# A fused attention and gated-FFN kernel on one core: where the closing waits stand, and when one add of the last block is planned

## The chip, the cores and the metric

The kernel runs on one core of a Trainium2 chip. A core has a matmul engine (PE; its weight loads are listed as PEld), a vector engine (DVE), an activation engine (ACT), GpSimd (POOL), and a sync engine (SP) that here issues every transfer between device memory (HBM) and the on-chip buffer (SBUF). Engines run their own instruction streams and meet at semaphores. The metric is the device time of one execution in microseconds (us), as the median of several runs.

## The reference

All tensors are bf16. `x` has 2048 rows of 576.

```python
x = A_x
xn = _layernorm(x, axis=-1)
s = _A_ref(xn, A_wqkv, A_wo)          # 32 heads of 18, causal, window of 256, softmax, then @ wo
g = _silu(_B_ref(xn, B_w_gate, B_w_up, B_w_down))
return x + s * g

def _B_ref(x, w_gate, w_up, w_down):
    g = jnp.einsum("bsd,df->bsf", x, w_gate)      # 576 -> 4608
    u = jnp.einsum("bsd,df->bsf", x, w_up)
    h = _sigmoid(g) * u
    return jnp.einsum("bsf,fd->bsd", h, w_down)   # 4608 -> 576
```

## The kernel before, in words

The 2048 rows go through in four chunks of 512 rows, each of four blocks of 128. For each chunk the program does: the layer norm on DVE; transposition, so that features lie on partitions (`xn`); the projection to q, k and v on PE (L460); attention in units of heads and keys (scores L589, exponential on ACT L607, masks on DVE L625, values L658); the output projection (L734), whose result ACT copies as a quarter of itself to `sat`; the FFN's two first matrices in 36 slices of 128 columns (L777), each followed by a tanh on ACT (L763) and a multiply on DVE (L767) into `hT`; and the FFN's second matrix, block by block (L851), accumulated over all 36 slices in PSUM.

A block ends in `final_cols` (from L904). Sigmoid and silu are made of tanh, and the factors of two are folded into scales. Four operations follow each other on a block's PSUM result y: ACT's tanh(y/4) into `thf` (L912, named fth), DVE's (t + 1) y (L914, fq1), DVE's product with `sat` (L916, fq2), and DVE's add of x in the tile `xf` (L918, fq3). Then SP stores `xf` to the output. The rows of x for `xf` are loaded anew by `load_xf`.

The last block of the last chunk has its own builder, `build_last` (L870). It makes the block in two column pieces, 0 to 448 (the large piece) and 448 to 576 (the small one): all 36 matmuls of the large piece, then all 36 of the small one (L881), each followed by its own `final_cols`, so its own four operations and its own store. Both pieces share one load of `xf`.

The order of the instructions on each engine is not written by hand. The builder makes a list of operations, each with an engine, an assumed duration, a priority and what it depends on. `schedule` (L924) is a planner: it repeatedly places, of the operations whose predecessors are placed, the one that can start first on its engine by the assumed times, with priorities as small penalties. The order of placing on an engine is the order of the program there. For a transfer the planner assumes an end by a bandwidth, and its `slack` is a further time that it adds before the operations that need the data count as ready. The slack is in no instruction; it moves only the plan. For the loads of `xf` it is LATE_SLACK, 5000 ns; the usual value for a transfer is DMA_SLACK_NS, 600 ns. SP's queue is planned in the same way.

`emit` (L1047) writes the program. Every transfer belongs to a lane, which is a semaphore of its own that rises by 16 per transfer; there are 84 lanes, one per ring buffer and kind of transfer. In front of each operation `run_engine` writes a wait for every semaphore that the operation needs and that the engine does not yet know to be high enough (`known`, kept per engine). The two stores of the last block are the last two transfers on SP; the large one goes through a lane that blocks before it used too, the small one through a lane of its own. At the end of SP's stream all 84 lanes are waited for, in a loop without regard to `known`:

```python
            if e == "SP":
                for ln, v in enumerate(lane_cnt):
                    if v > 0:
                        eng.wait_ge(lanes[ln], v)
                eng.nop()
```

In the built program these waits are mostly put two to an instruction: 41 wait instructions listed under L1095, one under L1096, and a single wait on the branch behind them (L1098). Then come a drain of each engine and a barrier of all of them.

Of the kernel before, what the change touches and what calls it, by code (L numbers as in the profile page):

```python
# [19 lines left out]
NFT = F // P  # L20
# [35 lines left out]
FB_CUTS = (0,3,6)  # L56
LAST = 448
W_GATE = 2
F2B = ((0, 1), (2, 3), (6, 7), (4, 5))
PVB = ((0,), (1,), (2,), (3,))  # L60

# [2 lines left out]
DMA_SLACK_NS = 600.0  # L64
# [8 lines left out]
LATE_SLACK = 5000.0  # L73
# [18 lines left out]
def mm_ns(n):  # L92
    return max(28.0, n / 2.4 + 2.5)
# [76 lines left out]
class Builder:  # L170
# [583 lines left out]
    def build_ffn(self, c):  # L754
# [82 lines left out]
        for blocks in (((0, 1), (2,), (3,)) if c == 0 else ((0,), (1,), (2,), (3,))):  # L837
            cands = F2B if blocks[-1] == QPC - 1 else ((6, 7), (4, 5), (0, 1), (2, 3))
            banks = {i: Psum(*cands) for i in blocks}
# [3 lines left out]
            for q in range(NWD):  # L843
                for i in blocks:
# [17 lines left out]
                    f2_ops[(i, q)] = o  # L862
                    if i == W_GATE and q == 0:
                        w_gate = o
# [5 lines left out]
    def build_last(self, c, prev):  # L870
        i = QPC - 1
        sb = c * QPC + i
        sth, dth = self.r_th.take()
        sx, o_x = self.load_xf(sb)
        for n, (c0, c1) in enumerate(((0, LAST), (LAST, D))):
            ps = Psum((6,), (7,), (4,), (5,), (0,), (1,), (2,), (3,))
            for q in range(NWD):
                def f_f2(e, q=q, ps=ps, c0=c0, c1=c1):
                    for fl in range(WDG):
                        ft = q * WDG + fl  # L880
                        r = e.matmul(self.bank(ps, c1 - c0), self.hT[:, ft, i * P:(i + 1) * P],  # L881
                                     self.wd_sb[:, q, fl, c0:c1], start=(ft == 0), stop=(ft == NFT - 1))
                    return r
                deps = [self.op_hT[ft] for ft in range(q * WDG, (q + 1) * WDG)] + [self.op_wd[q]]
                o = self.op("PE", WDG * mm_ns(c1 - c0), f_f2, f"f2:{sb}:{q}:{n}", deps, 3, alloc=[ps] if q == 0 else [],
                            mode="full", odeps=prev + ([self.op_wop[i - RTH]] if q == 0 else []))
                ps.users.append(o)
                prev = [o]
            ss, o_s = self.op_s[i]
            self.final_cols(sb, ps, o, sth, dth, ss, o_s, sx, o_x, c0, c1)  # L890

    def load_xf(self, sb):
        sx, dx = self.r_xf.take()
        return sx, self.dma(self.xf[:, sx, :], self.x[sb * P:(sb + 1) * P, :], P * D * 2, f"xf{sb}", ("xf", sx),
                            deps=dx + [self.op_hT[NFT - 6]], prio=3, slack=LATE_SLACK)

    def build_final(self, sb, ps, o_f2, sth, dth, ss, o_s):
        sx, o_x = self.load_xf(sb)
# [148 lines left out]
    def emit(self):  # L1047
        nc = self.nc
        ENGS = ("PE", "ACT", "DVE", "POOL", "SP")
        for o in self.ops:  # L1050
            if o.lane is not None:
                o.needs_tok = True
            for d in o.deps:
                d.needs_tok = True
        lanes = [nc.alloc_semaphore(f"lane{i}") for i in range(len(self.lane_ids))]
        lane_cnt = [0] * len(lanes)
        cnt = {e: 0 for e in ENGS}
        for e in ENGS:
            for o in self.prog[e]:
                if not o.needs_tok:  # L1060
                    continue
                if o.lane is not None:
                    ln = self.lane_ids[o.lane]
                    lane_cnt[ln] += 16
                    o.tok = (("L", ln), lane_cnt[ln])
                else:
                    cnt[e] += 1
                    o.tok = (("E", e), cnt[e])

        def semof(key):  # L1070
            return lanes[key[1]] if key[0] == "L" else self.sem[key[1]]

        def run_engine(e, eng):
            known = {}
            for o in self.prog[e]:
                waits = {}
                for d in o.deps:
                    k, v = d.tok
                    if e == "PE" and d.eng == "PE" and d is not o.fence:
                        continue  # L1080
                    if waits.get(k, -1) < v:
                        waits[k] = v
                for k, v in waits.items():
                    if known.get(k, -1) >= v:
                        continue
                    known[k] = v
                    eng.wait_ge(semof(k), v)
                ins = o.fn(eng)
                if o.needs_tok:
                    k, v = o.tok  # L1090
                    ins.then_inc(semof(k), 16 if o.lane is not None else 1)
            if e == "SP":
                for ln, v in enumerate(lane_cnt):
                    if v > 0:
                        eng.wait_ge(lanes[ln], v)  # L1095
                eng.nop()  # L1096

        with nc.Block() as block:  # L1098
            @block.tensor
            def _(eng):  # L1100
                run_engine("PE", eng)

            @block.scalar
            def _(eng):
                run_engine("ACT", eng)

            @block.vector
            def _(eng):
                run_engine("DVE", eng)

            @block.gpsimd
            def _(eng):
                run_engine("POOL", eng)

            @block.sync
            def _(eng):
                run_engine("SP", eng)
# [42 lines left out]
```

## Time and profile before

| what | value |
|---|---|
| time, median of 3 runs | 570.92 us (570.83 to 571.53) |
| the profiled execution, its own time | 571.24 us |
| its span, first to last instruction | 569.0 us |
| PE busy in the span | 560.6 us (99%) |
| DVE, ACT, POOL busy | 304.8, 274.7, 28.2 us |
| granted PE clock | 1.00 |
| DMA traffic | 73.03 MB, mean 128 GB/s |

Times in the profile are counted from the start of the span. A page cuts the span in 40 slices and gives each engine's busy share per slice in tenths. A timeline line has the start, the duration, the engine, the source line, the operation with what it writes and reads, and in brackets how long the engine was idle before it and who released it. "SPq" and the like mark an engine's sequencer: instructions that issue transfers, wait or branch, which do not count as busy time. "DMA to landing" is the time from the start of the issuing instruction to the last increment of its semaphore.

### The profile page before, as it was taken

How to read it: one execution, taken by the hardware profiler on the slowest of the kernel's cores; microseconds unless marked ns; L12 is line 12 of the kernel's file. 1: busy time of each engine (PE TensorE's matmuls, PEld its weight loads, DVE VectorE, ACT ScalarE, POOL GpSimd, SP SyncE). 2: the span in 40 equal slices, each digit the busy share in tenths (PEclk: the TensorE clock that was granted, in tenths of full speed). 3: DMA queues.
4: the chain of work that ended last, by engine and by line, in shares of the span. 5: the costliest groups of instructions: out<-in, count | busy, mean ns of one | idle time of the engine just before them, and what ended most of it. 6: DMA issues, size and time to landing. Idle time of an engine off the chain costs nothing.

```text
span 569.0 us, 17867 instructions
## 1 busy us (share of the span) xinstructions
PE 560.6 (99%) x7854; PEld 284.3 (50%) x7854; DVE 304.8 (54%) x664; ACT 274.7 (48%) x372; POOL 28.2 (5%) x55
## 2 busy tenths in 40 slices
PE   8999999999999999999999999999999999999996
PEld 5634444457544444456654444545754444444543
DVE  6137888732137896661205788765121586675312
ACT  7456666314055856721307576580321856856011
POOL 3000100010000100010000010001000000000100
PEclk9999999999999999999999999999999999999999
DMA  8999998528946765234694665604479455640001
GB/s 198 204 204 250 240 219 204 124 61 117 203 91 145 160 142 136 64 57 92 101 223 95 147 149 125 150 25 73 87 147 176 104 129 122 154 106 23 20 22 43
DMA packets 124874, 73.03 MB, mean 128 GB/s; under 512 B 53630, under 2 KB 124286, under 8 KB 124798
## 3 DMA queue, kind: packets, MB, share of 16 engines
q1 hardware_dynamic: 124798, 71.90, 59.5%
q8 instruction: 62, 1.02, 0.8%
q14 instruction: 14, 0.11, 0.1%
HBM read 55.22 MB, written 2.36 MB: 101 GB/s over the span
## 4 chain that ended last, share of the span: by engine, by line
PE 94%; SPq 2%; DMA 2%; issue 0%; ACT 0%; DVE 0%; DVEq 0%
PE ps L777 50%; PE ps L851 23%; PE ps L460 8%; PE ps L589 5%; PE ps L658 3%; PE ps L734 3%; SPq L210 2%; PE ps L881 2%; DMA wqkv_sb<-in_A_wqkv_dram 1%; DMA wgs<-in_B_w_up_dram 1%; ACT expr L509 0%; DVE xf L918 0%; DVE thf L914 0%; ACT thf L912 0%; DVE thf L916 0%
## 5 line engine op out<-in xcount | busy, mean ns | idle before, releaser
L777 PE MATMUL ps<-xn,wgs 64*128 64x512 bf16 x2592 | 298.8, 377 | 1.2 <-DMA wgs<-in_B_w_up_dram 1.1
L777 PEld LDWEIGHTS ps<-xn,wgs 64*128 64x128 bf16 x2592 | 120.8, 94 | 146.1 <-issue 9.8
L607 ACT ACTIVATE expr<-ps 128x1024 bf16<-128x1024 f32 x152 | 147.2, 1022 | 28.2 <-PE ps L589 28.2
L851 PE MATMUL ps<-wd_sb,hT 128*128 128x512 bf16 (+1 forms) x1080 | 134.4, 286 | 0.0
L763 ACT ACTIVATE tring<-ps 128x512 bf16<-128x512 f32 x144 | 86.3, 599 | 78.6 <-PE ps L777 63.6
L767 DVE SCALAR_TENSOR_TENSOR hT<-tring,ps 128x512 bf16<-128x512 bf16 x144 | 97.5, 677 | 28.5 <-PE ps L777 27.4
L851 PEld LDWEIGHTS ps<-wd_sb,hT 128*128 128x128 bf16 x1080 | 68.0, 98 | 65.7 <-DVE expr L625 1.7
L625 DVE TENSOR_TENSOR expr<-expr,m 128x512 bf16<-128x512 bf16 (+2 forms) x152 | 58.3, 412 | 61.8 <-ACT expr L607 61.0
L912 ACT ACTIVATE thf<-ps 128x576 bf16<-128x576 f32 (+2 forms) x17 | 10.6, 623 | 139.4 <-PE ps L851 132.2
L914 DVE SCALAR_TENSOR_TENSOR thf<-thf,ps 128x576 bf16<-128x576 bf16 (+2 forms) x17 | 12.2, 718 | 104.9 <-ACT thf L912 104.9
L460 PE MATMUL ps<-wqkv_sb,xn 64*128 64x288 bf16 x864 | 54.7, 283 | 0.6 <-DMA wqkv_sb<-in_A_wqkv_dram 0.6
L460 PEld LDWEIGHTS ps<-wqkv_sb,xn 64*128 64x128 bf16 x864 | 42.9, 94 | 11.3 <-issue 1.9
L589 PE MATMUL ps<-qkp 18*64 18x320 bf16 (+4 forms) x1472 | 32.4, 259 | 0.0
L589 PEld LDWEIGHTS ps<-qkp 18*64 18x64 bf16 x1472 | 16.1, 103 | 32.5 <-issue 15.7
L508 DVE CAST pk<-ps 128x576 bf16<-128x576 f32 x15 | 11.3, 755 | 23.0 <-PE ps L460 22.9
L698 DVE STREAM_TRANSPOSE op__63<-pk 128x512 bf16<-128x512 bf16 x32 | 22.3, 696 | 0.3
L636 POOL COPY qkp<-qkp 128x256 bf16<-128x256 bf16 x24 | 9.6, 398 | 248.6 <-PE ps L589 248.6
L676 DVE STREAM_TRANSPOSE pk<-ps 128x512 f32<-128x512 f32 x32 | 21.6, 675 | 0.0
L658 PEld LDWEIGHTS ps<-expr,vau 64*32 64x32 bf16 x1440 | 17.9, 92 | 6.4 <-issue 5.6
L658 PE MATMUL ps<-expr,vau 64*32 64x320 bf16 (+5 forms) x1440 | 20.7, 253 | 0.0
L674 DVE STREAM_TRANSPOSE tf<-ps 128x512 f32<-128x512 f32 x16 | 11.4, 713 | 15.4 <-PE ps L658 15.1
L734 PE MATMUL ps<-wo_sb,oT 64*128 64x512 bf16 (+1 forms) x288 | 18.7, 283 | 0.1
(52 smaller groups left out, 189.1 us busy)
## 6 DMA issues: line engine op xcount, KB each, us to landing
wgs<-in_B_w_gate_dram SPq DMA_DIRECT2D x48, 240.0 KB, 3.9
wgs<-in_B_w_up_dram SPq DMA_DIRECT2D x48, 240.0 KB, 4.7
wgs<-in_B_w_up_dram SPq DMA_DIRECT2D x48, 192.0 KB, 4.1
wgs<-in_B_w_gate_dram SPq DMA_DIRECT2D x48, 192.0 KB, 4.3
wd_sb<-in_B_w_down_dram SPq DMA_DIRECT2D x9, 576.0 KB, 6.3
xf<-in_A_x_dram SPq DMA_DIRECT2D x18, 144.0 KB, 2.2
out_dram<-xf SPq DMA_DIRECT2D x15, 144.0 KB, 1.9
xr<-in_A_x_dram SPq DMA_DIRECT2D x14, 144.0 KB, 4.2
```

The source lines that it names most:

```text
L460: r = e.matmul(self.bank(ps, HV, hf), self.xn[r0:r0 + 64, k, i * P:(i + 1) * P], self.wqkv_sb[r0:r0 + 64, j, k, :], start=(k == 0), stop=( ...
L589: r = e.matmul(self.ps[64 * half:64 * half + 64, b:b + n * 64], self.qkp[r0:r0 + DH, hg, k0:k0 + 64], self.qkp[r0:r0 + DH, hg, q0 * 64:(q0 ...
L607: return e.activation(self.expr[:, es, 2 * pr:2 * pr + 2, :], src, ACTF.Exp, scale=SM_SCALE)
L625: return e.tensor_tensor(ap, ap, m, ALU.mult)
L658: r = e.matmul(self.ps[32 * j:32 * j + 32, b + q0 * 64:b + (q0 + n) * 64], vf[:, v0:v0 + 32], self.expr[p0:p0 + 64, es, j, pos * 64:(pos + ...
L676: t3 = self.rd("DVE", dve_ns(CH), lambda e, tg=tg, hg=hg: e.transpose(tg, self.bank(ps2[hg][1])), f"t3:{c}:{hg}", deps=[o, self.last_mul] ...
L698: t2 = self.op("DVE", dve_ns(CH), lambda e, on=on: e.transpose(self.op_[:, hg % NOT, :], on.rearrange("p g d -> p (g d)")), f"t2:{c}:{hg}" ...
L734: r = e.matmul(self.bank(ps2[w], n1 - n0, n), self.oT[r0:r0 + 64, kt, qi * P:(qi + 1) * P], self.wo_sb[r0:r0 + 64, kt, n0:n1], start=(swap ...
L763: return e.activation(self.tring[:, st_, :], self.bank(ps), ACTF.Tanh, scale=0.5)
L767: return e.scalar_tensor_tensor(self.hT[:, ft, :], self.tring[:, st_, :], 1.0, self.bank(ps), ALU.add, ALU.mult)
L777: return e.matmul(self.bank((pg, pu)[gu][ft]), self.wgs[r0:r0 + 64, slots[ft // FG], i, fl * P:(fl + 1) * P], self.xn[r0:r0 + 64, i, :], s ...
L851: r = e.matmul(self.ps[:, b + n0:b + n1], lhsT, self.wd_sb[:, q, fl, n0:n1], start=(ft == 0), stop=(ft == NFT - 1))
```

## The change

It has two parts. First, on SP, the waits for all lanes but those of the last two stores (LAST_OUTS = 2) are written in front of the first of these stores, and noted in `known`. The loop at the end waits only for lanes that are not yet noted. Second, in `build_last` the load of `xf` has the slack DMA_SLACK_NS in place of LATE_SLACK, so that the planner takes its data to be ready 4400 ns earlier. In the built program this changes one place: on DVE the add of the large piece (L918) stands ahead of the small piece's L914 and L916, where before it stood behind them.

```diff
 LAST = 448
 W_GATE = 2
+LAST_OUTS = 2
@@ build_last
         sth, dth = self.r_th.take()
-        sx, o_x = self.load_xf(sb)
+        sx, o_x = self.load_xf(sb, DMA_SLACK_NS)
@@
-    def load_xf(self, sb):
+    def load_xf(self, sb, slack=LATE_SLACK):
         sx, dx = self.r_xf.take()
         return sx, self.dma(self.xf[:, sx, :], self.x[sb * P:(sb + 1) * P, :], P * D * 2, f"xf{sb}", ("xf", sx),
-                            deps=dx + [self.op_hT[NFT - 6]], prio=3, slack=LATE_SLACK)
+                            deps=dx + [self.op_hT[NFT - 6]], prio=3, slack=slack)
@@ emit
         def run_engine(e, eng):
             known = {}
+            end = [o for o in self.prog[e] if o.lane is not None][-LAST_OUTS:]
             for o in self.prog[e]:
+                if e == "SP" and o is end[0]:
+                    for ln, v in enumerate(lane_cnt):
+                        if v > 0 and not any(self.lane_ids[d.lane] == ln for d in end):
+                            eng.wait_ge(lanes[ln], v)
+                            known[("L", ln)] = v
                 waits = {}
@@
             if e == "SP":
                 for ln, v in enumerate(lane_cnt):
-                    if v > 0:
+                    if v > 0 and known.get(("L", ln), -1) < v:
                         eng.wait_ge(lanes[ln], v)
                 eng.nop()
```

## The prediction

> **What bounds the kernel now.** I read the engines and the 40 slices first: the matmul engine is busy for 560.6 of 569.0 us, at full clock, so the body belongs to it and neither edit touches an instruction of it. Only the last slice falls off. That slice is where the change acts, so I went on to the end of the span.
>
> ```profile
> span 569.0 us, 17867 instructions
> ...
> PE 560.6 (99%) x7854; PEld 284.3 (50%) x7854; DVE 304.8 (54%) x664; ACT 274.7 (48%) x372; POOL 28.2 (5%) x55
> ...
> PE   8999999999999999999999999999999999999996
> ...
> out_dram<-xf SPq DMA_DIRECT2D x1, 112.0 KB, 1.7
> ...
> out_dram<-xf SPq DMA_DIRECT2D x1, 32.0 KB, 1.6
> ```
>
> The timeline of the end comes next (columns: start, duration, engine, line, operation). PE ends at 563.96. Behind it run ACT, DVE and two stores, and the last one here is issued by 565.99. The span, however, ends at 569.0.
>
> ```profile
> 562.56 0.62 DVE L914 SCALAR_TENSOR_TENSOR thf<-thf,ps 128x448 bf16<-128x448 bf16 x1 [5.54 <-ACT thf L912]
> 562.79 1.17 PE L881 MATMUL ps<-wd_sb,hT 128*128 128x128 bf16 x18
> ...
> 563.22 0.39 DVE L916 TENSOR_TENSOR thf<-thf,sat 128x448 bf16<-128x448 bf16 x1
> 563.99 0.28 ACT L912 ACTIVATE thf<-ps 128x128 bf16<-128x128 f32 x1 [1.47 <-PE ps L881]
> 564.30 0.29 DVE L914 SCALAR_TENSOR_TENSOR thf<-thf,ps 128x128 bf16<-128x128 bf16 x1 [0.69 <-ACT thf L912]
> 564.62 0.22 DVE L916 TENSOR_TENSOR thf<-thf,sat 128x128 bf16<-128x128 bf16 x1
> 564.77 0.52 DVE L918 TENSOR_TENSOR xf<-xf,thf 128x448 bf16<-128x448 bf16 x2
> 565.18 0.81 SPq L210 DMA_DIRECT2D out_dram<-xf  x2
> ```
>
> The chain of waits says nothing of the 3 us behind that, since semaphore instructions do not count as busy. The view by source line shows them: first the closing waits (L1095, L1096), then the end of the program (L1098), with durations in ns and start times.
>
> ```profile
> L1095 SPq EVENT_SEMAPHORE  x41: 17/28/28, 566.0 to 568.5; - x41
> ...
> L1096 SPq EVENT_SEMAPHORE  x1: 28/28/28, 568.5 to 568.5; - x1
> ...
> L1098 SPq COMPARE_BRANCH  x1: 46/46/46, 568.6 to 568.6; - x1
> L1098 SPq DRAIN  x1: 13/13/13, 568.8 to 568.8; - x1
> ```
>
> The reader is to see a queue: 42 wait instructions on SP from 566.04 to 568.57, so 2.53/42 = 0.060 us from one to the next (28 ns is only their recorded part). The last store (issued 565.55) landed 1.57 us later, at 567.12. From then to 568.57, 1.45 us, SP only works off waits that have long been met. From the last of them to the end of the span (branch, drain, barrier of all engines) it is 569.01 - 568.57 = 0.44 us.
>
> The profiled execution took 571.24 us: its span of 569.01 and 2.23 around it. It stands 0.32 above the median of the runs, 570.92. I make the sum against the span and take the difference to the median.
>
> **Part 1, the add of the large piece.** In the built program the only instructions that change place are on DVE: the 448-column add (L918) now stands before the small piece's two operations. PE, ACT and POOL keep their order and their waits.
> - Its cost: the multiply before it ends at 563.22 + 0.39 = 563.61; 0.03 us is the gap between such neighbours (563.18 to 563.22 above); it takes 0.38 (0.52 for both adds, overlapped). So it runs from 563.64 to 564.03, in DVE time that is idle now (563.61 to 564.30; 0.69 in the row). The small piece's first DVE operation waits for ACT until 564.27 and keeps its 564.30, with 0.24 us of cover. Without that cover the small chain would move by what is missing, at most 0.38.
> - The add gets a second wait (the load of xf and the multiply; before, the token of the later multiply covered it). The extra instruction is one semaphore wait for the load, which stands ahead of the wait for the multiply and is met at 561.1; cost 0, or 0.06 if it is not decoded early.
> - What the last store gains: its add no longer stands behind the large one. It starts at 564.85 + 0.03 = 564.88 instead of 565.07, ends at 565.10 (0.22), and its store is issued 0.03 later, as the large one is now (565.15 to 565.18): at 565.13. Today it starts at 565.55, because SP is still at the large store (565.18 to 565.51). That is 0.43 earlier. The large store is now issued at 564.11 to 564.44, clear of it.
> - Landing: as the second of two stores back to back it takes 1.57. The pair of the block before shows what being second costs: 1.76 for the first, 1.88 for the second, and 0.34 against 0.43 for the issue. So alone I take 1.57 - 0.12 = 1.45 us; bounds are 1.45 and 2.16, the latter from the load of xf at 558.96, the slowest transfer of this stretch. I keep near the store rows, since they have the same direction and a like shape. Landing: 566.58.
>
> **Part 2, the waits ahead of the large store.** What moves is 82 of the 84 lanes' waits, two to an instruction, with the store's own wait for DVE in the last instruction: 41 of them stand between the load of xf (issued 558.96, SP free at 559.30) and the large store. Queued behind them on SP are only the two stores; no other engine waits for SP there, and no transfer is issued between.
> - The 22nd waits for that load's lane and is met when it lands, 558.96 + 2.16 = 561.12. By pace it would be reached at 559.3 + 21 x 0.06 = 560.6, so SP stands 0.5 us there. 19 more at 0.06 follow: done at 562.3. The add that the large store needs ends at 564.03. So the cover is 1.7 us, and before the last store is touched another 565.13 - 564.44 = 0.69 us. I cost the moved waits at nothing; if every one of the 19 cost 0.06 us more, still nothing, with 0.15 each the cover is just used up.
> - What is left at the end: one wait instruction for the small store's lane, and the other lane's wait on the branch, whose store lands near 564.11 + 1.7 = 565.8. SP goes on about 0.02 us after a landing (the load of xf was issued at 558.96, the landing that it waited for was at 558.94), 0.03 for the wait, then the 0.44 of before: 566.58 + 0.05 + 0.44 = 567.07.
>
> **The sum.** 569.01 - 567.07 = 1.94 us off the span. Apart: the add alone would let the queue of waits begin at 565.13 + 0.33 = 565.46 instead of 565.99, 0.53 off; the waits alone would give 567.12 + 0.05 + 0.44 = 567.61, 1.40 off. 570.92 - 1.94 = 568.98, said as 569.0, 0.34% faster.
>
> A rule of the Trainium skill speaks against so quick a landing: "DMA: Bandwidth & Descriptors", section "Anatomy of one DMA", gives about 2.0 us of fixed cost for a transfer, most of it the receipt of the write, though measured on the other way of issuing (by GpSimd). By that figure, as an estimate, the small store would land at 565.13 + 2.08 = 567.21 and the gain would be 1.31 us (569.61). The trace of before has 1.57 for this very store, so I go by the trace.
>
> **The rivals.**
> 1. *The store's landing takes the place of the waits.* If the lone small store takes the 2.16 us of the load, the end is 565.13 + 2.16 + 0.05 + 0.44 = 567.78, 1.23 off: 569.7. For it: once the waits are gone, the landing ends last with no cover at all. Against it: every store of the last 25 us landed in 1.6 to 1.9, and DMA is nearly idle (0.17 of the 16 engines at the end).
> 2. *The add does not help, the waits do.* If the small chain is held up by the large add (its cover is 0.24 us) or the stores meet anyway, only the 1.40 is left: 569.5. Against it: 0.38 of work goes into a hole of 0.69.
> 3. *Slower: the moved waits hold up the large store.* Its place is SP between 561.12 and 564.03. Behind it the last store follows at 0.43 us, then landing (1.57) and closing (0.49). To end 1.14 us after 569.01 the large store would have to start at 570.15 - 0.49 - 1.57 - 0.43 = 567.66: the 19 waits would cost (567.66 - 561.12)/19 = 0.34 us each. Then 572.1. Against it stand 42 such waits in a row at 0.060.
> 4. *The body drifts.* Another program on other addresses; the three runs of before lie 0.7 us apart. If that eats half the gain, the time is 570.0, nearer to no change than to a measurable one.
>
> **How the numbers follow.** This kernel's measurement tells about 0.2%, 1.14 us, from no change. My forecast (both parts work; 568.4 to 569.4) 0.60, rival 2 0.14, rival 1 0.10, rival 4 0.12, rival 3 0.04. Faster by over 0.2% (below 569.78): forecast, rival 2, and nearly all of rival 1, which lies at the bound with its 569.7 (0.08 of 0.10): 0.82. Same: rival 4 and the rest of rival 1: 0.14. Slower: 0.04. The range reaches down to 568.3 (the forecast with the runs' spread of 0.7 below the middle) and up to 569.9, which takes in rivals 1 and 2 and leaves out most of 4 and all of 3, near 0.17 with the lower tail.
>
> **What would show it.** Right: the semaphore instructions of the closing waits stand between 559 and 562.5 us, one is left behind the last store; the 448-column add starts near 563.6, right after its multiply; the large store's issue is near 564.1, the small one's near 565.1 with 0.33 us of its own; the span is near 567.1 and ends 0.5 us after the last landing. Wrong: a gap of SP between the last moved wait and a DVE add already done (rival 3); the small piece's first DVE operation more than 0.05 after its activation (rival 2); a landing near 2.1 us (rival 1); PE's end away from 563.96 by more than 0.3 us (rival 4), which would make the prediction wrong without touching its steps.

## The result, and the profile after

The changed kernel takes 569.5 us (median of 22 runs, 568.31 to 572.41) against 570.95 us (22 runs of before, 570.31 to 572.1). The ratio is 0.9975 with a 95% interval of 0.9966 to 0.9985, so 0.25% or 1.4 us faster. The profiled execution took 569.1 us with a span of 566.9.

The timeline of its end, from the large piece's activation on (columns as before):

```profile
561.82 0.54 ACT L913 ACTIVATE thf<-ps 128x448 bf16<-128x448 f32 x1 [5.72 <-PE ps L882]
...
563.05 0.39 DVE L917 TENSOR_TENSOR thf<-thf,sat 128x448 bf16<-128x448 bf16 x1
563.47 0.39 DVE L919 TENSOR_TENSOR xf<-xf,thf 128x448 bf16<-128x448 bf16 x1
563.83 0.28 ACT L913 ACTIVATE thf<-ps 128x128 bf16<-128x128 f32 x1 [1.47 <-PE ps L882]
563.96 1.34 SPq L211 DMA_DIRECT2D out_dram<-xf  x2
564.14 0.29 DVE L915 SCALAR_TENSOR_TENSOR thf<-thf,ps 128x128 bf16<-128x128 bf16 x1 [0.27 <-ACT thf L913]
564.46 0.23 DVE L917 TENSOR_TENSOR thf<-thf,sat 128x128 bf16<-128x128 bf16 x1
564.72 0.23 DVE L919 TENSOR_TENSOR xf<-xf,thf 128x128 bf16<-128x128 bf16 x1
```

The 448-column add now follows its multiply at once and ends 0.27 us before the small piece needs DVE. The two stores, which stood back to back within 0.81 us, now spread over 1.34.

The view by source line of the same kernel (moved waits L1081, one more together with the store's own wait for DVE L1094, the wait left at the end L1103, the end of the program L1105):

```profile
L1081 SPq EVENT_SEMAPHORE  x40: 27/28/28, 559.2 to 562.1; - x40
...
L1094 SPq EVENT_SEMAPHORE  x1: 27/27/27, 563.9 to 563.9; - x1
...
L1103 SPq EVENT_SEMAPHORE  x1: 17/17/17, 566.4 to 566.4; - x1
...
L1105 SPq COMPARE_BRANCH  x1: 46/46/46, 566.5 to 566.5; - x1
L1105 SPq DRAIN  x1: 12/12/12, 566.7 to 566.7; - x1
```

and of the small store alone (L211):

```profile
L211 SPq DMA_DIRECT2D out_dram<-xf x1: 332/332/332, 565.0 to 565.0; - x1
...
DMA to landing us min/median/max: 1.5/1.5/1.5
```

Forty wait instructions have gone into the time in which SP only stood by, and the one left at the end follows the small store's landing (issued 564.97, landed 566.43 by the trace's landing times, 1.46 us) within 0.02 us.

To compare runs I take the *tail*: from the start of the small piece's activation, the last one on ACT, to the end of the span. It leaves out all that happens ahead of it. It was 569.01 - 563.99 = 5.02 us and is 566.91 - 563.83 = 3.08 us. That is 1.94 less, the size that was forecast. The medians, however, lie only 1.45 apart. So there were two questions: do the two parts give what the sum said, and does the body ahead of the tail take 0.5 us back?

| kernel | small piece's activation starts | tail | ratio to before, 95% interval |
|---|---|---|---|
| before | 563.99 | 5.02 | |
| before, again | 563.76 | 5.02 | 0.9996 (0.9983 to 1.0008) |
| changed | 563.83 | 3.08 | 0.9975 (0.9966 to 0.9985) |
| changed, again | 563.68 | 3.07 | 0.9967 (0.9953 to 0.9980) |
| changed, a third time | 563.84 | 3.08 | 0.9965 (0.9952 to 0.9977) |
| waits only | 563.13 | 3.67 | 0.9969 (0.9955 to 0.9983) |
| add only | 564.38 | 4.50 | 0.9992 (0.9980 to 1.0003) |
| waits ahead of the last store alone | 563.90 | 4.90 | 1.0002 (0.9984 to 1.0021) |
| half of the waits moved | 564.14 | 3.20 | 0.9969 (0.9957 to 0.9980) |

Each ratio is against runs of before that were taken alongside.

### The profile page after: what moved, and what is told of

The parts are those of the page before. It is cut to its first block, busy times and chain, and to the rows that moved or that the text cites. A ratio compares the mean times of both kernels' runs of the same rounds, so it can differ in the third digit from the quotient of the medians.

```text
span 566.9 us, 17841 instructions
## 1 busy us (share of the span) xinstructions
PE 557.1 (98%) x7827; PEld 283.8 (50%) x7854; DVE 305.4 (54%) x664; ACT 274.7 (48%) x372; POOL 28.2 (5%) x55
## 4 chain that ended last, share of the span: by engine, by line
PE 97%; issue 1%; DMA 1%; ACT 1%; SPq 1%; DVE 0%
PE ps L778 51%; PE ps L852 23%; PE ps L461 9%; PE ps L590 5%; PE ps L659 3%; PE ps L735 3%; PE ps L882 2%; DMA wqkv_sb<-in_A_wqkv_dram 1%; SPq L211 1%; ACT sat L750 0%; ACT expr L608 0%; ACT expr L510 0%; PE ps L440 0%; ACT tring L764 0%; DVE thf L915 0%
## 5 line engine op out<-in xcount | busy, mean ns | idle before, releaser
L852 PE MATMUL ps<-wd_sb,hT 128*128 128x64 bf16 (+1 forms) x1053 | 130.9, 284 | 2.7 <-issue 1.7
L509 DVE CAST pk<-ps 128x576 bf16<-128x576 f32 x15 | 11.3, 755 | 23.0 <-PE ps L461 22.9
```

What stands on the lines that cost most here:

```text
L852: r = e.matmul(self.ps[:, b + n0:b + n1], lhsT, self.wd_sb[:, q, fl, n0:n1], start=(ft == 0), stop=(ft == NFT - 1))
```

## The experiments

### Each part alone

The waits only: the changed kernel with the load's slack as before.

```diff
-        sx, o_x = self.load_xf(sb, DMA_SLACK_NS)
+        sx, o_x = self.load_xf(sb)
```

> The 82 waits moved, the add left where it was. Tail theory (tail: from the start of the small piece's activation to the end of the span; 5.02 us before, 3.08 in the changed kernel): the stores go out as before, back to back, the small one lands 1.57 us after its issue, and the end follows 0.49 us later: tail 3.62, so 1.40 us less than before. If the body of the program does not move, the time is 1.40 us (0.25%) below before. Rival, body theory: moving the waits also makes what lies ahead of the tail 0.5 us longer on average and more spread (the changed kernel's median is 1.45 us down where its tail is 1.94 down): then the time is only 0.9 us (0.16%) down with the same tail of 3.62, and the runs spread by more than 2 us.

The tail is 566.80 - 563.13 = 3.67 (3.62 expected). From the timeline of its end:

```profile
563.13 0.28 ACT L913 ACTIVATE thf<-ps 128x128 bf16<-128x128 f32 x1 [1.47 <-PE ps L882]
563.44 0.29 DVE L915 SCALAR_TENSOR_TENSOR thf<-thf,ps 128x128 bf16<-128x128 bf16 x1 [0.70 <-ACT thf L913]
563.76 0.22 DVE L917 TENSOR_TENSOR thf<-thf,sat 128x128 bf16<-128x128 bf16 x1
563.90 0.52 DVE L919 TENSOR_TENSOR xf<-xf,thf 128x448 bf16<-128x448 bf16 x2
564.38 0.81 SPq L211 DMA_DIRECT2D out_dram<-xf  x2
```

DVE's hole of 0.70 and the pair of stores in 0.81 are those of before. The 0.05 that the sum missed is in the first step of SP: the large store is issued 0.09 us after its add ends (564.29 to 564.38), and 0.03 after it in the kernel before, since one more wait instruction stands between. The ratio, 0.9969, is at least as good as the 0.9975 that 1.40 us would give. The 0.9984 of the theory that moving the waits costs 0.5 us of body lies just outside its interval.

The add only: before, with the diff of `load_xf` and `build_last` alone.

> The add of the large piece planned first, the closing waits left at the end. Tail theory: the small store is issued 0.43 us earlier and its issue takes 0.33 instead of 0.43, so the queue of 42 waits starts 0.53 us earlier and ends 0.53 earlier: tail 4.49, time 0.53 us (0.09%) below before. Rival, the add is worth nothing by itself as the waits hide it: tail 5.02. Body theory: if the extra 0.5 us of body comes with the other order of the adds, the time is equal to before with a tail of 4.49.

The tail is 4.50 (4.49 expected), so the add is worth 0.52 us even with all waits left. From its views by line and its timeline of SP:

```profile
564.45 1.41 SPq L210 DMA_DIRECT2D out_dram<-xf  x2
```

```profile
L1095 SPq EVENT_SEMAPHORE  x41: 17/28/28, 565.9 to 568.3; - x41
```

The 41 waits begin 1.5 us after the small piece's activation (564.38) where they began 2.05 after it, and they end the program as they did. In time it is not told from no change (0.9980 to 1.0003), and 0.09% could not be. The two parts sum to 1.35 + 0.52 = 1.87 against 1.94 for both: when the stores are apart, the extra wait ahead of the large one no longer delays the small one, so that beside the moved waits the add is worth 3.67 - 3.08 = 0.59.

### The two kernels once more

> The changed kernel once more, unchanged. Tail theory with a body that only scatters: tail 3.08 to within 0.05, start of the small piece's activation anywhere from 563.5 to 565, time 1.94 us (0.34%) below before within its interval. Body theory: time about 1.4 us (0.25%) below before again, spread of the runs again about twice that of before.

> The kernel before, unchanged, timed against itself. Both theories: ratio 1.000. What it tells: how far the ratio of two equal programs strays here, how much the runs spread (0.5 us of standard deviation so far), and how far the start of the small piece's activation moves from one profile to the next (563.99 in the one profile) with a tail of 5.02.

> The changed kernel a third time, for the size: tail 3.08 to within 0.05. If the 1.94 us of the tail are all there is, ratio 0.9966 within its interval; if the body of the changed program is longer by 0.5 us, ratio 0.9975 for a third time and the start of the small piece's activation is later than 564.2.

All three profiles of the changed kernel have a tail of 3.07 or 3.08, both of before have 5.02. What differs between profiles, of the same program too, is when the tail begins: 563.13 to 564.38 over the nine. The begin of the scatter can be read from ACT's first copy of projected keys (L509, into a buffer named `expr`). From the timelines of ACT, before:

```profile
20.93 0.65 ACT L509 ACTIVATE expr<-ps 128x576 bf16<-128x576 f32 x1 [3.39 <-PE ps L460]
```

and the same program again:

```profile
20.55 0.65 ACT L509 ACTIVATE expr<-ps 128x576 bf16<-128x576 f32 x1 [2.85 <-PE ps L460]
```

At 21 us they are already 0.38 apart. Over the nine profiles ACT's 41st activation starts between 51.22 (waits only) and 52.28 (add only), a scatter of 1.06 us:

```profile
51.22 0.60 ACT L764 ACTIVATE tring<-ps 128x512 bf16<-128x512 f32 x1
```

```profile
52.28 0.60 ACT L763 ACTIVATE tring<-ps 128x512 bf16<-128x512 f32 x1
```

From there to the small piece's activation it is 511.91 to 512.17 in each, a scatter of 0.26. So the body's scatter comes mostly from the first 52 us. In that stretch DMA is near full (8 or 9 tenths in the first four slices of the page of before), and the chain that ended last waits 6.75 us for `wqkv_sb` and 4.75 us for `wgs`; that these waits are what scatters is not shown.

The changed kernel's body is not later than that of before in the profiles (563.83, 563.68, 563.84 against 563.99, 563.76), and behind the 41st activation it is not longer (511.91 to 511.99 against 511.96 and 512.17). Its three ratios, 0.9975, 0.9967 and 0.9965, lie on both sides of the 0.9966 that 1.94 of 570.95 us gives; the interval of each reaches it, the first only with its edge. So no profile shows a body that is 0.5 us longer, and the second and third ratio do not repeat it. The times alone do not refute it, since the 0.9975 lies within all three intervals. That the 0.5 us of the first comparison is scatter of the start is the likelier reading, but it is not shown. The wide spread of the first comparison (4.1 us) did not come back either: it was 1.6 us the second time and 1.1 the third, with fewer runs.

### Where the waits stand

One number is changed, so that the waits stand one transfer later, between the two stores:

```diff
-LAST_OUTS = 2
+LAST_OUTS = 1
```

> The changed kernel with the closing waits one transfer later: ahead of the last store alone (LAST_OUTS = 1), so between the two stores. Theory (SP's waits are a queue of 0.06 us each, free only where SP has nothing to issue): the large store still goes out 0.13 us after the small piece's activation starts, SP is free 0.33 later, then 42 wait instructions take 2.55, and the small store, ready at 1.14 after the activation's start, goes out only at about 3.05; it lands 1.46 later, and the end follows 0.45 after that: tail about 4.95 against 3.08 of the changed kernel and 5.02 of before, so time the same as before (ratio 0.999 to 1.000). Rival, a wait that is met costs nothing and what helped was having the waits ahead of any store: tail 3.1 to 3.2, ratio 0.997.

Nearly all of the gain is gone: the tail is 4.90 (4.95 expected) against 5.02 before, the ratio 1.0002. From its timeline:

```profile
558.88 0.34 SPq L211 DMA_DIRECT2D xf<-in_A_x_dram  x1
563.97 3.29 SPq L211 DMA_DIRECT2D out_dram<-xf  x2
...
564.79 0.22 DVE L919 TENSOR_TENSOR xf<-xf,thf 128x128 bf16<-128x128 bf16 x1
```

the second of its two stores alone, and the view by line:

```profile
566.92 0.33 SPq L211 DMA_DIRECT2D out_dram<-xf  x1
```

```profile
L1081 SPq EVENT_SEMAPHORE  x41: 17/28/28, 564.4 to 566.8; - x41
...
L1094 SPq EVENT_SEMAPHORE  x1: 28/28/28, 566.9 to 566.9; - x1
```

The small store's data is ready at 565.02, and SP issues the store at 566.92, after 42 wait instructions whose starts keep an even pace of 0.06 us, so that none of them had to be waited for. The rival, that a met wait costs nothing, falls: they cost 0.06 us each, and nearly the same instructions cost nothing one transfer earlier, between 558.88 and 563.97, where SP has nothing to issue.

### Half of the waits

```diff
-                        if v > 0 and not any(self.lane_ids[d.lane] == ln for d in end):
+                        if v > 0 and ln % 2 and not any(self.lane_ids[d.lane] == ln for d in end):
```

> The changed kernel with only the lanes of odd number waited for ahead of the two stores; 21 wait instructions stay behind the last store. Theory (waits cost only what they last beyond the landing): the small store goes out 1.14 us after the activation's start, SP is free at 1.47, 21 instructions at 0.06 end at 2.8, the store lands at 2.60 and the wait for its lane is the last but one: tail 2.8 + 0.44 = 3.2, at most 0.2 above the changed kernel, ratio 0.997. Rival, each wait left behind costs its 0.06 in full: tail 3.08 + 1.26 = 4.3, ratio 0.9988.

The tail is 3.20, 0.12 above the changed kernel, with a ratio of 0.9969. Its waits behind the last store, from the view by line, the loop (L1102) and the last of them (L1103):

```profile
L1102 SPq EVENT_SEMAPHORE  x20: 28/28/28, 565.7 to 566.8; - x20
```

```profile
L1103 SPq EVENT_SEMAPHORE  x1: 28/28/28, 566.9 to 566.9; - x1
```

They run while the store is under way (issued 565.29, landed 566.75), and only the end of the queue, to 566.90, lies behind the landing. A wait behind the last store costs only what it lasts beyond the landing: of the 42 in the kernel before, the last 24 did, 23 of L1095 and the one of L1096 (567.12 to 568.57, 0.06 us each).

## Why the prediction was right

The forecast was 569.0 us, with a range of 568.3 to 569.9 and faster; measured 569.5.

- **What bounds the end.** Right. The span ended on a queue of met waits on SP, and with the queue gone the last landing takes its place: 566.43 to the wait's start at 566.45 and the span's end at 566.91, 0.48 us, where the sum had 0.05 + 0.44.
- **Part 1, the add.** Right in each step. Counted from the small piece's activation, the large add ends 0.04 after it starts (forecast 0.04), the small piece's first DVE operation keeps its 0.31 (564.14 - 563.83), and the small store is issued 1.14 after it (565.13 - 563.99 = 1.14 forecast). The store alone takes 0.33 to issue, and lands 1.46 us after it (1.45 forecast). The fixed 2.0 us that the Trainium skill gives for a transfer issued by GpSimd ("DMA: Bandwidth & Descriptors", section "Anatomy of one DMA") does not carry over to this store, which SP issues; the trace's 1.46 decides.
- **Part 2, the waits.** Right: SP stood at the load's lane (one wait at 560.43, the next at 560.97), as forecast with 0.5 us, and had worked off the rest by 562.1, 1.7 us ahead of the end of the large add. What was left out is the 0.07 us that the wait instruction right in front of the large store adds between the add and the store; it costs nothing since the small store comes 0.7 later.
- **The sum.** 1.94 us forecast, 1.94 in the tail. The step that was off is the last one, from the sum to the median: it took the body to be equal in the median, and the first comparison leaves 0.5 us of the tail's gain out. Repeated, the gain is 0.33% and 0.35%; where the 0.5 us went is open. The scatter of the first 52 us had its place in rival 4 (the body drifts) and in the range, not in the middle.
- **The rivals.** The landing did take the place of the waits, but in 1.46 us, not 2.16. That only the waits help fell: the add is worth 0.52 alone and 0.59 beside the moved waits. It is luck of the number that speaks for this rival: its 569.5 is the very median that was measured, and without the tail the time would have been read as its proof. The slower one, waits that hold up a store, has its mechanism confirmed by the run with the waits one transfer later, at 0.06 us each and not 0.34; where the change put them there was cover for it.

## What to carry to other kernels

Instructions that wait for semaphores long met still pass one by one on their queue, and a profile that leaves them out of busy time shows them only as a span that goes on behind the last work. Put them where the issuing engine has nothing to do, ahead of the last transfers, and leave only those for the last transfers behind; ask what is queued behind them, as one place later they cost nearly all that they had given. Where a gain is smaller than the run-to-run scatter of a start-up phase, measure it from a late event to the end of the span, which here repeated to 0.01 us while the gain by the ratios went from 0.25% to 0.35%, 0.6 us.

## What the runs showed of the hardware

Met wait instructions on SP start every 0.060 us though only 0.028 of each is recorded, and one can hold two semaphores (42 instructions for 83 lanes in the kernel before). The small store, issued right behind the large one, takes 0.43 us to issue and 1.57 to land; apart from it 0.33 and 1.46. Keeping the two stores apart was worth 0.1 us on each count. The 1.46 is the same whether the large store is still under way (changed kernel: issued 564.97, the large one landed at 565.65) or has landed long before (waits ahead of the last store alone: 566.92 and 565.66), so it is the issue right behind that costs, not the transfer beside it. Over the nine profiles of these nearly equal programs the first 52 us scatter by 1.06 us, the 512 us behind them by 0.26.
